# One-tile first block, raw-weight Q and K, split first scores and gate tiles moved into attention

## The chip, the cores and the metric

The kernel runs on one core of a Trainium2 chip. The metric is the device time of one execution in microseconds (us). A core has five instruction queues that run side by side and meet at semaphores: PE (TensorE: matmuls; PEld is its weight load, which overlaps the matmuls), ACT (ScalarE), DVE (VectorE), POOL (GpSimd) and SP (SyncE, which here issues DMAs only). Each queue executes in its own order. Matmul results go to PSUM, which the kernel uses as eight banks of 128 x 512 float32; ACT and DVE evacuate them from there to SBUF.

## The reference

One transformer-like block on 2048 tokens of width 448: adaptive layer norm, sliding-window attention with 16 heads of width 28 (window 256), then a second adaptive layer norm and a gated MLP whose gate mixes tokens with a 2048 x 2048 matrix.

```python
mod = silu(c) @ w_mod                      # 6 vectors of 448: sa ca ga sb cb gb
h = layernorm(x) * (1 + ca) + sa
q, k, v = split(h @ wqkv)                  # 16 heads of 28
s = q @ k.T * 28 ** -0.5                   # causal, |q - k| < 256
x = x + ga * ((softmax(s) @ v) @ wo)
h = layernorm(x) * (1 + cb) + sb
z = gelu(h @ w_in)                         # 1792 wide
z1, z2 = z[:, :896], layernorm(z[:, 896:])
g = w_sp @ z2 + b_sp[:, None]              # w_sp: 2048 x 2048
x = x + gb * ((z1 * g) @ w_out)
```

## The kernel before

Tokens are cut into 16 tiles of 128. The work is described as small operations (names below), each with its engines, dependencies and the buffers or PSUM banks it takes. `ORDER`, a string of operation numbers, fixes the order of issue on every queue and the choice of engine and bank; nothing is scheduled at run time. Waits follow from dependencies and from buffer reuse.

**Loads.** All on SP's queue except c and one half of the first modulation weights, which ACT's queue issues. Weights with 448 rows are held as four chunks of 128 rows that overlap (`load_dup`, rows 0, 128, 192 and 320), with half of chunk 2 zeroed in the Q, K and V weights (memsets `zv`, `zqk`).

**First layer norm and projections.** Tiles are taken in blocks: `'blocks': (2, 2, 2, 2, 4, 4)`. For each block `ln1` takes statistics (DVE, L543 to L550), the inverse root on POOL (L551) and the normalised tile xn (L565 on DVE, L564 on POOL, L594 on ACT). The first four blocks are transposed by PE (`transp_pe`) and evacuated with the modulation applied: hT, two chunks of 256 columns per operation pair (ACT L622, DVE L626). The last two blocks are transposed by DMA (`transp_dma`, L641) and modulated afterwards (L633). The modulation columns modT come from 32 one-column matmuls (`mod_cols`) on the first load of w_mod. `project` then runs, per block, eight chains of four matmuls for Q and K (QKT, heads in four groups of 32-row slots), evacuated at L718 (ACT) or L721 (DVE), and one chain of four per tile for V (Vaug, L729 or L732). The Q and K weights are first copied from wqk_raw into WQK with each head widened from 28 to 32 columns (`wqkp`, L657 and L658, eight copies over three engines); every chain of Q and K waits for such copies.

**Attention.** Query tile j meets key tiles j-2, j and j-1. For each pair one group of 16 matmuls (K = 28, four row groups side by side) writes scores S for all 16 heads into two pairs of banks (bank pairs (0,1), (2,3), (4,5)). Two exponentials (ACT L796, 128 x 1024) each read a pair of banks and write a PT buffer; POOL masks where needed (L804); eight PV matmuls per PT buffer accumulate the output in bank 6. Then rec and nrm (DVE), a DMA transpose to oT, four `wo` matmuls, and x1 (DVE L842). There are 90 exponentials. Banks 6, 7, 4 and 5 (`d_banks`) also serve the projection chains, so scores and projections share banks 4 and 5.

**Gate.** The second layer norm works on x1 in pairs of tiles (h2, by DMA transpose). z2 of a tile is seven passes of 448 columns (`Pair`: six full matmuls and two half-height ones that run side by side), evacuated by the gelu (L899), which needs another ACT table than the exponential. Tiles in `'zraw': (0, 1)` are evacuated without gelu (`z2e`, L892) into z2 and get the gelu later from SBUF (L895). z1 is computed transposed (L918). In the order of this kernel all z1 and z2 matmuls stand behind the last score.

**Mixing.** G: 448 matmuls of 512 columns with the DMA-transposed w_sp, then `ga`, `gu` (DVE), 112 output matmuls, `fin` and the stores.

PE also gets 44 `warm` matmuls of 256 columns and 64 of 128 columns on 32-column groups (16 at a time), on zeros, where the order has nothing else for it; 11 of the 44 stand behind the first score.

Of the kernel before, what the change touches and what calls it, by code (L numbers as in the profile page):

```python
# [55 lines left out]
class Planner:  # L56
# [108 lines left out]
0 16 7 1 21 20 17 18 26 23 28 27 118 120 2 3 1673/0 1674 1675 1676 1677 1678 1679 1680 1681 1682 1683 1684 1685 29/2 1686 1687 1688 1689 1690 1691  # L165
1692 1693 1694 25 30 1695 32/1 33 34 31 8 9 14 6 10 5 4 12 15 13 11 50 119 51 121 54 52 122 53 19 22 55 123 24 56 58/0 124 57 125.2/4 126.2/1 35 1696
1697 1698 1699 1700 36 37 1701 60/0 38 1702 1703 39 59/3 127/0 131/2 40 41 49 46 45 48 47.1 128 61 62.1 63.1 65/1 1704 64 1705 1706 132 1707 1708 1709
66 67 134 129.1 130.1 42 43 44 323 319 321 325 324 326 320 322 327 93/3 88/7 98/0 89 90 103/2 104 99 100 101 91 94 83/1 105 68/6 69 106 70 84 102 92
107 133 85 71 78/7 86 79 95 96 80 81 87.1 72 97 73/0 74 82 75 76 113/6 114 115 116 252 185 77 487/0,1 488/3 491/6 328 329 330.1/1 117.1 333.1/4
332.1/3 489 492 331.1/2 1710 108/4 109 110 1711 140/1 111 141 142 1712 1713 143 145/0 146 147 1714 1715 1716 148 502/1,0 112 155/2 156 157 158 186 254  # L170
253 255 187 402 188 189 404 159.1 403 256 144 149 485/1 135/0 136 1717 137 138 1718 165/2 166 167 168 506/0 503/1 486 509/0,1 139 169 493/0 490 170/2
171 1719 1720 172 180/1 181 182 183 173 160/3 161 162 163 510/7 512/9 184 522/0,1 150/1 151 152 153 494 495/1 257 258 507 504 190 408 406 174.1 191
334 336 337 496/1 335 154.1 505/0 513 511 508 407 514 515/2 405 164 526/10 523/3 529/1,2 530/7 192.1/3 193.1/0 259.1/4 175/1 176 177 178 179.1 516/0
533/1 194/0 195 409 196 197 536/0,1 198/1 199 200.1 201.1 222/3 497/2 498 499 500 207/0 223 208 209 210 224 202/1 203 225 539/4 537/5 211 226 549/0,1
553/8 550/6 260.1/1 531 410 501 932 265/2 204 205 206.1 212/3 232/0 213 214 215 233 266 234 235 216.1 517/1 518 519 520 227/3 521 534 524 411 412 554
527 413.1/3 415.1/0 236 268 267 556/1,0 560/0 557/9 228 229 230 538/0 237/2 217/1 525 238 239 231.1 934 218 219 262/3 261 220 240 532 535 340 241.1
221 264.1 263.1 563/1,0 540 528 564/2 566/4 269/1 242/3 314/2 243 270 315 316 317 244 245 576/1,0 541 933 935 542/2 318.1 936 246.1 577/5 580/3 294/0
295 271 272 296 247/2 297 279/3 248 249 280 281 250 273.1 274/1 275 276 282 277 419 543/1 903 900 902 901 298.1 283.1 278.1 251 583/1,0 284/0 299/2
300 301 302 285 286 287 584/7 587/10 303.1 289/1 290 291 292 288.1 590/1,2 591/1 416.1/2 561 558 414.1/1 551 418 339.1 937 341.1 567/0 555 552 938
293.1 939/2 581 578 941/0 588 585 338.1 559 565 562 593/6 603/1,0 544/1 545 546 547 607/8 604/4 568 569/2 548 917/0 918 919 920 921 922 610/2,0 611/9  # L180
# [43 lines left out]
"""  # L224

PARAMS = {
    'blocks': (2, 2, 2, 2, 4, 4),
    'by_pe': (1, 1, 1, 1, 0, 0),
    'ln1': (-40, -30, 0.3, 3.633, 3.0, 6.5),
    'tr': (-40.674, 0.2, 0.83, 0.9, 3.1, 2.821),  # L230
    'pj': (-38.951, 0.3, 0.8, 1.6, 4.0, 7.776),
    'st': (0.1, 0.1, 0.2, 0.22, 0.407, 0.505),
    'gateA': 0.5,
    'modB': -0.497,
    'gateB': 15.054,
    'pv': -0.964,
    'wo': -19.98,
# [33 lines left out]
def dve4_ns(n):  # L271
    return 225 + n / 3.84
# [811 lines left out]
```

## Time and profile before

| | us |
|---|---|
| runs of the kernel | 282.6, 280.43, 279.98 |
| median of the runs | 280.43 |
| span of the profiled execution | 279.1 |
| busy: PE, PEld | 268.0, 142.8 |
| busy: DVE, ACT, POOL | 156.1, 135.4, 94.2 |
| 90 exponentials on ACT | 84.4 |
| first score, last score (start, PE) | 17.32, 109.89 |
| first exponential, end of the last one | 17.77, 112.5 |
| last matmul ends | 276.3 |

The span runs from the first to the last instruction of one profiled execution; the runs are timed separately and lie a little above it. Busy time is the union of an engine's instructions. A matmul is drawn to its modelled end, so two matmuls back to back overlap in the drawing (a 512-column matmul is drawn 379 ns long), and the distance from start to start in a dense run tells more than a duration does. The granted clock of TensorE was 1.00 in all stretches but the last 20 us, where it was 0.99.

### The profile page before, as it was taken

What the parts mean: (1) busy time and instruction counts of PE and PEld (TensorE: products, weight loads), DVE (VectorE), ACT (ScalarE), POOL (GpSimd) and SP (SyncE); (2) the same over time, 40 slices, a digit from 0 to 9 for tenths busy, and PEclk for the clock granted to TensorE, in tenths of its full rate; (3) what the DMA queues carried; (4) which work ended last, traced back from release to release, by engine and by line L of the source; (5) the groups of instructions that cost most, each with busy time, mean ns of one, the idle gap of its engine ahead of it and who ended that gap; (6) DMA issues with size and microseconds to landing.
All of it is one profiled execution on the core that took longest, in us unless ns stands there. A gap on an engine that the chain in (4) does not pass through costs nothing.

```text
span 279.1 us, 6498 instructions
## 1 busy us (share of the span) xinstructions
PE 268.0 (96%) x2750; PEld 142.8 (51%) x2776; DVE 156.1 (56%) x373; ACT 135.4 (49%) x183; POOL 94.2 (34%) x156
## 2 busy tenths in 40 slices
PE   8899999999999988999999999999999999999995
PEld 4667677655565645444344444444444444444452
DVE  5688775576757688597385841332424230433543
ACT  4689999999999999866566600000000000000000
POOL 4166796755568677646322120000000000000000
PEclk9999999999999999999999999999999999999999
DMA  7954129796587683469999700000000000000223
GB/s 240 366 125 76 23 42 203 131 168 161 145 152 133 126 154 77 94 113 169 172 167 189 133 4 0 0 2 0 0 0 0 19 0 0 2 0 0 66 79 105
DMA packets 67503, 25.38 MB, mean 91 GB/s; under 512 B 56337, under 2 KB 67346, under 8 KB 67474
## 3 DMA queue, kind: packets, MB, share of 16 engines
q1 hardware_dynamic: 67200, 24.50, 42.5%
q8 instruction: 22, 0.36, 0.6%
q10 hardware_dynamic: 274, 0.46, 0.5%
q14 instruction: 7, 0.06, 0.1%
HBM read 9.48 MB, written 1.84 MB: 41 GB/s over the span
## 4 chain that ended last, share of the span: by engine, by line
PE 79%; ACT 16%; DMA 2%; issue 1%; DVE 1%; SPq 0%
PE ps L435 79%; ACT PT L796 13%; DMA wmod_sb<-in_w_mod_dram 2%; ACT hT L622 2%; ACT QKT L718 1%; SPq L466 0%; DVE fin L1005 0%; DVE x_sb L842 0%; DVE st_all L543 0%; ACT Vaug L729 0%
## 5 line engine op out<-in xcount | busy, mean ns | idle before, releaser
L796 ACT ACTIVATE PT<-ps 128x1024 bf16<-128x1024 f32 x90 | 84.4, 1078 | 2.6 <-PE ps L435 2.3
L986 DVE TENSOR_TENSOR tmpg<-ps,bsp_bc 128x512 bf16<-128x512 f32 x28 | 19.3, 691 | 59.2 <-PE ps L435 59.2
L435 PE MATMUL ps<-QKT,z 128*128 128x512 bf16 x219 | 50.7, 379 | 0.3
L804 POOL TENSOR_SCALAR_AFFINE_SELECT PT<-PT 128x512 f32<-128x512 f32 x60 | 37.2, 638 | 11.3 <-ACT PT L796 11.3
L435 PE MATMUL ps<-hT,WQK 128*128 128x256 bf16 (+1 forms) x182 | 34.6, 305 | 2.2 <-ACT hT L622 0.8
L435 PEld LDWEIGHTS ps<-QKT,z 128*128 128x128 bf16 x224 | 21.9, 98 | 26.4
L551 POOL TENSOR_TENSOR rs_all<-ve_all,neghalf 128x1 f32<-128x1 f32 (+2 forms) x31 | 20.0, 650 | 38.1 <-DVE ve_all L550 37.8
L435 PE MATMUL ps<-w_in_sb,hT 128*128 128x448 bf16 (+1 forms) x128 | 29.2, 353 | 0.1
L435 PE MATMUL ps<-hT,w_in_sb 128*128 128x512 bf16 (+1 forms) x106 | 27.5, 379 | 0.5 <-DVE st_all L543 0.3
L435 PE MATMUL ps<-w_spC,z 128*128 128x512 bf16 x110 | 26.7, 379 | 0.1
L435 PE MATMUL ps<-w_spD,z 128*128 128x512 bf16 x109 | 26.1, 379 | 0.2
L435 PEld LDWEIGHTS ps<-Vaug,PT 128*128 128x128 bf16 x720 | 22.7, 97 | 5.8 <-ACT PT L796 0.4
L435 PE MATMUL ps<-Vaug,PT 128*128 128x29 bf16 x720 | 25.0, 176 | 0.5 <-POOL PT L804 0.2
L543 DVE BATCH_NORM_STATS2 st_all<-z2raw 128x6 f32<-128x448 bf16 x32 | 18.6, 615 | 10.4 <-ACT z2raw L899 10.3
L435 PEld LDWEIGHTS ps<-hT,WQK 128*128 128x128 bf16 x192 | 16.9, 97 | 10.8 <-ACT hT L622 1.8
L435 PE MATMUL ps<-w_out_sb,z1T 128*128 128x448 bf16 x112 | 22.3, 352 | 0.0
L633 POOL TENSOR_SCALAR hT<-hT,modT 128x256 bf16<-128x256 bf16 (+1 forms) x31 | 18.5, 601 | 10.8 <-DMA hT<-xn 10.8
L564 POOL TENSOR_SCALAR xn<-x_sb,rs_all,nm_all 128x512 bf16<-128x512 bf16 x23 | 17.5, 769 | 8.0 <-DVE nm_all L555 4.3
L543 DVE BATCH_NORM_STATS2 st_all<-x_sb 128x6 f32<-128x448 bf16 x32 | 18.9, 615 | 1.7 <-DMA x_sb<-in_A_x_dram 1.5
L435 PE MATMUL ps<-QKT 28*128 28x128 bf16 x720 | 18.1, 217 | 1.7 <-ACT PT L796 1.3
L721 DVE CAST QKT<-ps 128x256 bf16<-128x256 f32 (+1 forms) x27 | 14.2, 531 | 8.3 <-PE ps L435 7.9
L918 ACT ACTIVATE z1T<-ps 128x512 bf16<-128x512 f32 x28 | 15.6, 600 | 5.8 <-PE ps L435 5.7
(70 smaller groups left out, 273.3 us busy)
## 6 DMA issues: line engine op xcount, KB each, us to landing
wmod_sb<-in_w_mod_dram SPq DMA_DIRECT2D x8, 224.0 KB, 4.0
w_in_sb<-in_B_w_in_dram SPq DMA_DIRECT2D x8, 224.0 KB, 3.8
out_dram<-fin SPq DMA_DIRECT2D x16, 112.0 KB, 1.7
x_sb<-in_A_x_dram SPq DMA_DIRECT2D x3, 448.0 KB, 8.3
wqk_raw<-in_A_wqkv_dram SPq DMA_DIRECT2D x2, 452.0 KB, 7.3
bsp_bc<-in_B_b_sp_dram SPq DMA_DIRECT2D x1, 512.0 KB, 5.8
x_sb<-in_A_x_dram SPq DMA_DIRECT2D x2, 224.0 KB, 3.3
wmod_sb<-in_w_mod_dram ACTq DMA_DIRECT2D x1, 448.0 KB, 4.5
```

Source lines behind the costliest of these rows:

```text
L435: return e.matmul(out_, lhsT=lhsT, rhs=rhs, start=st, stop=sp, **kw)
L543: st = [dve("%sst%d" % (name, i), prio, dve_ns(D), lambda e, i=i, s_=s_: e.bn_stats(st_all[:, slot, t, i, :], s_()), deps, tens) for i, s_ ...
L551: r = pool(name + "rs", prio, 420 + 148 * n, lambda e: e.tensor_tensor(rs_all[:, slot, t0:t1], ve_all[:, slot, t0:t1], neghalf[:, t0:t1], ...
L564: return e.tensor_scalar(dst, src, rs_all[:, slot, t:t + 1], nm_all[:, slot, t:t + 1], ALU.mult, ALU.add)
L622: return e.activation(hT[:, c_, cols], ps[:, ten.slot, q * 256:q * 256 + 256], ACT.Identity, bias=modT[:, c_:c_ + 1], scale=modT[:, 4 + c_ ...
L633: return e.tensor_scalar(hT[:, c_, cols], hT[:, c_, cols], modT[:, base_col + 4 + c_:base_col + 5 + c_], modT[:, base_col + c_:base_col + ...
L718: return e.activation(QKT[:, g, cols], ps[:, ten.slot, 0:w], ACT.Copy)
L721: return e.tensor_copy(QKT[:, g, cols], ps[:, ten.slot, 0:w])
L796: e_op = P.op("E%d_%d" % (j, ui), pr, [("act", 925, lambda e, ten=ten, pt=pt: e.activation(PT[:, pt.slot, :, :], ps[:, ten.slot:ten.slot + ...
L804: ready = pool("M%d_%d" % (j, ui), pr - 50, pool_ns(512), lambda e, pt=pt, pat=pat, cm=cm, cmp=cmp: e.affine_select(out=pt32(pt.slot), in_ ...
L918: g = P.op("z1g%d_%d" % (tb, ft), pr - 19, [("act", act_ns(512), lambda e: e.activation(z1T[:, ft, tb * 512:(tb + 1) * 512], ps[:, ten.slo ...
L986: a = dve("ga%d_%d" % (tb, ft), pr, dve_ns(512), lambda e, tb=tb, ten=ten, tg=tg: e.tensor_tensor(tmpg[:, tg.slot, :], ps[:, ten.slot, :], ...
```

## The change

Nine things are changed together, and `ORDER` is a new one throughout.

1. Blocks are 1, 1, 2, 4, 4 and 4 tiles instead of 2, 2, 2, 2, 4 and 4. PE transposes the first three (tiles 0 to 3), DMA the rest, so tiles 4 to 7 now come by DMA.
2. All weights of 448 rows in the first half lie in four chunks of 112 rows, without overlap (`load_112`, R1 = 112); xn is written in four chunks of 112 with 16 columns of padding, zeroed once (`xpad`). The memsets `zv`, `zqk` and the copies of c fall away. The loads of x are 1, 3, 4, 4 and 4 tiles; wqk is loaded ahead of wv; on ACT's queue the half of wmod stands ahead of c.
3. Q and K of the first block are made from wqk_raw without the widening copy: each matmul of a chain becomes four with 32 columns of weights, one for each column group (`raw_chain`).
4. A widening copy waits for its half of wqk_raw only.
5. For j = 0 the scores come in two halves of eight matmuls, for head groups (0, 1) into banks 0 to 3 and (2, 3) into banks 4 to 7, each with its own exponential.
6. hT chunks are evacuated per transposed bank; in the first two blocks 112 x 128 each.
7. `zraw` is tiles 0 to 4 instead of 0 and 1, and ordering constraints that kept gate work behind certain scores are dropped. By the new order z2 of tiles 0 to 3 stands ahead of the last score.
8. All 44 warm matmuls now stand ahead of the first score.
9. In attention ACT has eight 512-column copies of QKT instead of five.

```diff
-    'blocks': (2, 2, 2, 2, 4, 4),
-    'by_pe': (1, 1, 1, 1, 0, 0),
+    'blocks': (1, 1, 2, 4, 4, 4),
+    'raw': (1, 0, 0, 0, 0, 0, 0),
+    'by_pe': (1, 1, 1, 0, 0, 0),
...
-    'zraw': (0, 1),
+    'zraw': tuple(range(5)),
...
-    x0 = load_x("x0", -99, 0, 2)
-    t_wmA = load_dup("wmodA", -98, wmod_sb, w_mod, 0, 2 * D, engs=("sp", "act"), rate=290.0)
-    t_wv = load_ov("wv", -97, wv_sb, A_wqkv, 2 * D, 3 * D, o=2 * D)
-    x1 = load_x("x1", -96, 2, 2)
-    t_wqk = load_dup("wqk", -95.5, wqk_raw, A_wqkv, 0, 904)
+    x0 = load_x("x0", -99, 0, 1)
+    t_wmA = load_112("wmodA", -98, wmod_sb, w_mod, 0, 2 * D + 16, engs=("sp", "act"))
+    t_wqk = load_112("wqk", -97, wqk_raw, A_wqkv, 0, 904)
+    x1 = load_x("x1", -96, 1, 3)
+    t_wv = load_112("wv", -95, wv_sb, A_wqkv, 2 * D, 3 * D, o=2 * D)
...
+        def raw_chain(g):
+            ten = Ten(B_D if b else B_ALL, guard=True)
+            ops = []
+            for k in range(4):
+                def fn(e, k=k):
+                    last = None
+                    for r in range(4):
+                        a = 112 * g + DH * r
+                        last = mm(e, ps[32 * r:32 * r + 32, ten.slot, 0:w], wqk_raw[0:R1, k, a:a + 32], hT[0:R1, k, cols],
+                                  k == 0, k == 3, tile_position=(0, 32 * r))
+                    return last
+                ops.append(pe("qk%d_%d_%d" % (b, g, k), 0, mm_ns(w), fn, [t_wqk[k // 2], hT_op[b][k]], [ten], order=ops[-1:], mode=33))
...
+                s_ops = []
+                halves = [[Ten(banks((a, a + 1))) for a in a_] for a_ in ((0, 2), (4, 6))] if j == 0 else [tens]
+                for gs, tens in zip(((0, 1), (2, 3)) if j == 0 else ((0, 1, 2, 3),), halves):
+                    deps = [QK_op[(g, blk[j])] for g in gs] + [QK_op[(4 + g, blk[kb])] for g in gs]
+                    s_ops.append(pe("S%d_%d%s" % (j, ui, "h%d" % gs[0] if j == 0 else ""), pr - 50, 270,
+                                    lambda e, j=j, kb=kb, tens=tens, gs=gs: s_mm(e, j, kb, tens, gs), deps, tens, mode=32, order=all_S[-1:]))
...
-                    [pair.ops], [joint, zt], table="gelu", order=[prev_e])
+                    [pair.ops], [joint, zt], table="gelu")
```

More of the change, by code (lines that the diff above doesn't have):

```diff
@@ L602, in transp_pe @@
         hT_op[b] = [None] * 4
-        for half in range(2):
+        per = 1 if b == 0 else 2
+        for u in range(4 // per):
             ten = Ten(B_ALL if b == 0 else B_D, guard=True)
@@ L799, in bass_adaLN_cond__sliding_block__mixer_gmlp__prompt_kernel @@
+            S_op[(j, ui)] = s_ops[-1]
+            e_op = P.op("E%d_%d" % (j, ui), pr, [("act", 925, lambda e, e_in=e_in, e_out=e_out: e.activation(
+                e_out(), e_in(), ACT.Exp, scale=SCALE))], [s_op, t_exp0], e_tens + [pt], table="exp")
             E_op[(j, ui)] = e_op
-            e_op.scores = -1
             ready = e_op
```

323 lines of the change are left out of this document (162 added, 161 removed), and 4 rows, old and new, of the table PARAMS.

## The prediction

> **What bounds the kernel now.** I read the stages first (busy time of each engine in chosen stretches; the numbers after the range are its length, then busy us and instruction counts of PE, PEld, DVE, ACT, POOL, then clock, DMA share, GB/s).
>
> ```profile
> 17.30:30.00 12.70, 12.22 (x213) 8.64 (x213) 11.13 (x30) 12.06 (x18) 10.39 (x16) 1.00 0.35 66
> 30.00:75.00 45.00, 43.91 (x817) 28.70 (x826) 30.91 (x73) 43.66 (x54) 30.39 (x47) 1.00 0.66 127
> 75.00:95.00 20.00, 18.98 (x410) 11.67 (x404) 12.57 (x29) 19.88 (x23) 13.40 (x22) 1.00 0.70 134
> 95.00:105.00 10.00, 8.97 (x196) 5.47 (x194) 8.65 (x16) 9.56 (x11) 8.15 (x15) 1.00 0.90 161
> 105.00:110.60 5.60, 4.76 (x125) 3.49 (x122) 4.71 (x12) 5.54 (x7) 4.09 (x7) 1.00 0.37 77
> 110.60:160.00 49.40, 49.03 (x283) 21.16 (x288) 33.92 (x93) 33.23 (x52) 20.82 (x35) 1.00 0.83 147
> 160.00:276.30 116.30, 115.73 (x543) 53.86 (x551) 42.10 (x85) 0.45 (x1) 1.58 (x3) 1.00 0.04 14
> ```
>
> TensorE (PE) is full almost everywhere: it stands still 1.6 us from 17.3 to 75, 2.9 us from 75 to 110.6, 0.9 us after that. ACT is as full as PE until 110. So time comes off in three ways: an earlier start, less PE work, or filling PE's 2.9 us. The chain of waits (start, length, what) agrees: late in attention it runs over the exponentials, after it over PE alone.
>
> ```profile
> 80.62 23.95 ACT PT L796 x26
> ...
> 110.56 5.83 PE ps L435 x57
> 116.39 0.05 issue
> 116.44 9.28 PE ps L435 x49
> ```
>
> The start, from the timeline (start, length, engine, line, instructions, and in brackets the idle time before and its releaser):
>
> ```profile
> 7.99 0.47 PEld L435 LDWEIGHTS ps<-sc_sb,wmod_sb 128*128 128x128 bf16 x16 [1.01 <-DMA wmod_sb<-in_w_mod_dram]
> 10.62 0.63 ACT L658 ACTIVATE WQK<-wqk_raw 128x512 bf16<-128x512 bf16 x1 [1.02 <-DMA wqk_raw<-in_A_wqkv_dram]
> 11.15 3.28 ACT L622 ACTIVATE hT<-ps,modT 128x256 bf16<-128x256 f32 x7
> 14.49 2.14 PE L435 MATMUL ps<-hT,WQK 128*128 128x256 bf16 x18 [0.56 <-ACT hT L622]
> 17.32 0.40 PE L435 MATMUL ps<-QKT 28*128 28x128 bf16 x16
> 17.77 1.94 ACT L796 ACTIVATE PT<-ps 128x1024 bf16<-128x1024 f32 x2 [0.72 <-PE ps L435]
> ```
>
> The modulation weights land at 7.95, ACT evacuates seven of the eight hT chunks one after another until 14.4, the first score is at 17.32, the first exponential at 17.77.
>
> **Paces used**, from dense runs of the timeline: 512 columns 0.216 us (28 matmuls from 168.57 to 174.61); 448 columns 0.19 (8 from 91.20 to 92.81); 256 columns 0.110 (18 in 2.14, less one drain of 0.17); 128 columns 0.056 (10 transposes in 0.72, less the drain); PV 0.027 (48 from 93.15 to 94.53); 16 scores 0.34, and about 0.1 to enter them (four 512-column matmuls took 0.99 ahead of a score, not 0.87).
>
> **1. The first score comes earlier: -4.0 us (-4.7 to -2.7).** Each half of wmod is 408 KB instead of 459 KB behind the same x bytes; 6.14 us of flight scale to 5.5, so it lands near 7.4, not 7.95. 32 one-column matmuls (16 took 0.55) and two copies of 0.15 give modT at 9.0. crow now goes out behind wmod on ACT's queue: that half took 4.5 us from issue, so c is there near 5.5, the silu near 6, the table load of 1.28 ends by 7.6; hidden, as nothing needs ACT before xn1. On DVE, a copy of wqk_raw stands ahead of hT; it needs the first half only. Before, both halves were there at 10.62; the bytes say the first at 9.1 to 10, I take 9.4. Then copy (0.27), modT, three 128-column evacuations: no row has that width; 0.23 (half of the 256-column 0.46) to 0.46, taken 0.34: hT of tile 0 complete at 10.7, its second weight half at about 10.3. Twenty raw groups of four 32-column matmuls follow. The nearest row is the warm-up's: 16 such weight loads in 0.35, 0.55 until the next kind starts; so 80 cost 1.75 to 2.75 us, taken 1.9. With twelve 128-column matmuls (0.7) the half score starts at 13.3. The same row says that a 32-column load at 22 ns is nearly as dear as the full 128-column load of PV at 30. [...]
>
> **2. PE's work from there on: +1.6 us (+1.1 to +2.9).** Q and K before: 96 x 0.110 + 64 x 0.216 = 24.4. After: 12 raw groups (0.09 each) + 20 x 0.056 + 32 x 0.110 + 96 x 0.216 = 26.5. Four more V matmuls fall behind the first score, +0.8; eleven warm-ups no longer do, -1.2; eight transposes fewer, -0.4; three mode changes, +0.3. The upper end takes raw groups at 0.14 and mode changes at 0.4 (the weight-load gap at a warm-up batch).
>
> **3. Waits that the start adds: +1.7 us (+0.5 to +3.5).** The second half score takes all four projection banks (4 to 7). It needs chains for g = 2, 3, 6, 7, one of which waits for the first exponential to free bank 2 (near 15.0) and another for ACT's copy behind that exponential; so it runs near 16.6. By 16.0 ACT has done its two hT chunks of tiles 2 and 3 (0.46 each) and then waits about 1 us. Behind it PE's queue holds one V chain, then K of tile 1, which needs the second exponential to finish (18.0); score 1 needs that K's copy: 19.2. From 15.0 to 19.2 PE has 2.8 us of work: 1.4 us lost. Next, tiles 4 to 7 come by DMA transpose now: statistics on DVE until 17.8, the 4-wide rstd on POOL 1.0, four normalisations of 0.77 until 22.4, four transposes on SP (three took 4.45 to issue, each 2.8 to land), two modulations of 0.77 on POOL: 28.5; PE reaches them at 27.7. With 0.8 there and 0.5 of old idle (12.70 - 12.22), +1.7.
>
> **4. Four gate tiles in attention: -3.6 us (-4.3 to -2.9).** The program says five tiles; by the order of instructions, 32 of 128 matmuls, four tiles, stand ahead of the last score, the fifth behind it. Per tile 6 full and 2 half-height matmuls, 7 x 0.19 = 1.33, so 5.3 us leave the stage after the last score and 16 PV matmuls (0.4) enter it. In attention these 5.3 us fill idle time: 2.9 by the table; up to 4.3 when the runs from 75 to 110 are priced by the paces, as the drawn end of a matmul hides part of a wait. What fits is gain, the rest only changes place. Their eight evacuations (0.55 to 0.62; one on ACT, seven on DVE, which was 8.65 of 10 busy from 95 to 105) lie beside this; the w_out scaling there (3.7 us of DVE) is earlier in the new order. Without that cover each late evacuation would hold a bank, 0.6 us.
>
> **5. Two full engines side by side: +0.6 (0 to 2).** ACT has 1.0 us more evacuations within attention (eight 512-column copies for five, five Vaug for three). At tile 13 the replay puts PE at 95.5 and ACT at 95.6; engines so equal wait for each other.
>
> Cleaned-up orders, 112-row layouts and the moved memsets leave matmul counts as they are: 0. Output and everything from 160 on are unchanged: 0.
>
> **Sum:** -4.0 + 1.6 + 1.7 - 3.6 + 0.6 = -3.7 us against the profiled span of 279.1: 275.4. The median of the runs, 280.43, is 1.3 above that span; the forecast is 276.7.
>
> **Rivals.**
> A, the start gives all back: PE waits 4 us more instead of 1.7 before tile 3, since banks 4 to 7 and the second exponential hang together. For: it's a ring of waits through one engine each. Against: PE has V and projections to do. 276.7 + 2.3 = 279.0. Chance 0.13.
> B, the gate matmuls don't fit: they stand in the last six score periods, where PE gets 13.4 us of work against 11.0 of exponentials, and idle time before 98 can't take them. Term 4 shrinks to -0.3: 280.0. Chance 0.12.
> C, PE has more room than its busy row shows, and ACT alone sets attention: ACT waits for PE only 1.7 us in 17 to 105 and weight loads fill just 55 to 68% of attention. Then the last exponential moves with the first (-4.0, +1.0) and the tail is 4.9 shorter: 280.4 - 7.9 = 272.5. Against: priced by paces, 17 to 75 has under half a us free. Chance 0.12. [...]
> D, slower: the four DMA transposes serialise. Before, POOL waited up to 4.0 us for DMA hT<-xn. First issue 20.9, four landings of 2.8 one after another, modulation: 33.7, against PE at 27.7; PE's queue is in order, so scores 2 and 3 wait behind and ACT starves: 6.0 instead of 0.8, 276.7 + 5.2 = 281.9. Every us after 27.7 costs one; it decides against the change from 31.5 on. Chance 0.13.
>
> **How the numbers follow.** The forecast has 0.50. About 1% (2.8 us) is what a measurement here can tell from no change: faster means under 277.6. Of the forecast's 0.50, 0.38 lie there and 0.12 within 1%, with 274.5 to 279 as its own range. C adds 0.12 to faster and A 0.02; A (0.11), B (0.09) and D (0.01) add to the same; B (0.03) and D (0.12) to slower. Faster 0.52, same 0.33, slower 0.15. The range 273.0 to 280.8 takes in A, B and the low bounds of terms 1 and 4, and leaves out most of C and D.
>
> **What would show it.** First score at 12.6 to 14.6 (1). PE idle from first score to 30 about 2 us (3). Last score near 111, and 161.5 us from it to the end instead of 166.4 (4). PE idle under 1.5 us in the last 35 us of attention, with ACT now waiting for PE there. A first score after 15, or a PE wait of over 3 us for DMA-transposed hT near 28, would make the prediction wrong.

## The result, and the profile after

The changed kernel is slower: 290.19 us median of four runs (287.1, 290.94, 289.77, 290.6) beside 281.44 for the kernel before on the same chip (282.6, 280.43, 279.98, 282.44); ratio 1.030, 95% interval 1.023 to 1.037. The forecast was 276.7. The profiled run is the quickest of the four: 287.1 us, span 285.4, against 279.1 before.

The stages after (busy time of each engine in chosen stretches, columns as before; the first and the last but two borders are the first and the last score):

```profile
16.37:30.00 13.63, 12.86 (x233) 8.75 (x232) 12.11 (x32) 12.31 (x23) 6.74 (x12) 1.00 0.40 93
30.00:75.00 45.00, 43.23 (x759) 24.54 (x755) 30.41 (x75) 41.38 (x49) 31.77 (x48) 1.00 0.58 96
75.00:95.00 20.00, 18.58 (x358) 10.70 (x357) 13.67 (x26) 17.34 (x19) 7.94 (x14) 0.91 0.68 142
95.00:105.00 10.00, 8.39 (x162) 4.54 (x160) 7.23 (x12) 8.93 (x11) 7.07 (x12) 0.83 0.79 146
105.00:121.33 16.33, 14.91 (x276) 8.69 (x273) 11.83 (x28) 12.61 (x15) 11.69 (x20) 1.00 0.35 60
121.33:160.00 38.67, 38.12 (x251) 16.56 (x255) 30.73 (x86) 27.95 (x43) 16.20 (x26) 1.00 0.69 137
160.00:282.60 122.60, 121.95 (x576) 56.56 (x585) 49.84 (x102) 5.49 (x8) 3.27 (x6) 1.00 0.21 41
```

Three readings. First, the balance: the first score comes at 16.37 instead of 17.32 (-0.95), first to last score takes 105.0 instead of 92.6 (+12.4), and from the last score to the end it is 161.2 instead of 166.4 (-5.2); sum +6.3. Second, PE stands still 7.0 us between first and last score (length less busy, five rows), 4.2 before; and ACT, full before, waits 11.3 us for PE (2.3 before). Third, the clock column, 1.00 in every row before, is 0.91 and 0.83 from 75 to 105.

The start, from the timeline:

```profile
11.75 3.46 DVE L650 COPY WQK<-wqk_raw 112x512 bf16<-112x512 bf16 x4
...
11.89 1.18 PE L437 MATMUL ps<-hT,wqk_raw 112*32 112x128 bf16 x70 [0.27 <-DVE hT L617]
12.32 2.75 POOL L543 TENSOR_SCALAR xn<-x_sb,rs_all,nm_all 128x448 bf16<-128x448 bf16 x2
...
15.28 0.34 PE L437 MATMUL ps<-hT,wqk_raw 112*32 112x128 bf16 x10 [2.21 <-issue]
...
16.92 1.04 ACT L827 ACTIVATE PT<-ps 128x1024 bf16<-128x1024 f32 x1
```

The 80 raw matmuls begin at 11.89; after 70 of them, in the middle of a group of four, PE stands still for 2.21 us with no releaser ("issue"). In the same time one of DVE's widening copies takes 2.49 us, where the copy before it and the two behind it take 0.28, and POOL's two normalisations take 0.72 and 2.05 us.

Late in attention, the chain of waits (start, length, what), which before ran over the exponentials there:

```profile
81.35 0.39 DVE x_sb L871
81.74 4.33 DMA hT<-xn
...
86.16 0.72 DVE xn L543
86.88 0.57 DVE hT L626
87.45 0.54 DVE x_sb L871
...
88.04 8.09 PE ps L437 x132
```

DVE's queue is in order. A normalisation of the second layer norm (tile 5) waits at its head until a DMA transpose has read the buffer it needs; behind it stands x1 of tile 7, which frees the bank for PE's V matmuls. PE waits 1.42 us. The same happens on POOL at 116.0 (a modulation waiting for a transpose, a mask behind it, 1.42 us); at 99.06 PE waits 1.43 us for ACT. What follows such a wait shows in stretches of 3.41 us:

```profile
86.11:89.52 3.41, 1.99 (x52) 1.24 (x49) 3.12 (x6) 2.24 (x4) 1.26 (x3) 1.00 0.73 179
89.52:92.93 3.41, 3.41 (x65) 1.89 (x62) 1.33 (x4) 2.58 (x3) 0.00 (x0) 0.50 0.46 74
...
113.41:116.83 3.42, 2.00 (x33) 1.00 (x32) 2.15 (x6) 2.39 (x4) 2.03 (x4) 1.00 0.55 52
116.83:120.24 3.41, 3.41 (x81) 2.15 (x80) 2.69 (x5) 1.85 (x3) 3.41 (x6) 1.00 0.19 38
```

Behind the wait at 88.0 (and the one at 99.1) the granted clock is 0.50 for 3.41 us: by an estimate half of that time, 1.7 us, is lost each time. Behind the wait at 116, as long, it stays at 1.00. The runs of the kernel before test the price: in the sessions below 24 of them had a mean clock of 0.999 or 1.000 and took 280.40 us on average, 17 had 0.994, which is what one such stretch gives, and took 282.07, so 1.67 us more. The other runs of the changed kernel had mean clocks of 0.970, 0.982 and 0.970; by the same estimate, (1 - clock) x span, they lost 5 to 9 us in this way, the profiled one 3.4.

### The profile page after: what moved, and what is told of

It reads as the page before. It is cut to its first block, busy times and chain, and to the rows that moved or that the text cites. A ratio compares the mean times of both kernels' runs of the same rounds, so it can differ in the third digit from the quotient of the medians.

```text
span 285.4 us, 6678 instructions
## 1 busy us (share of the span) xinstructions
PE 270.2 (95%) x2840; PEld 139.1 (49%) x2856; DVE 165.8 (58%) x385; ACT 132.9 (47%) x177; POOL 93.0 (33%) x150
## 4 chain that ended last, share of the span: by engine, by line
PE 77%; DMA 8%; POOL 5%; DVE 5%; ACT 2%; issue 2%; SPq 0%; DVEq 0%; POOLq 0%
PE ps L437 77%; DMA hT<-xn 5%; DMA x_sb<-in_A_x_dram 2%; ACT PT L827 2%; POOL PT L833 2%; DVE st_all L522 2%; POOL xn L543 1%; DMA oT<-o_sb 1%; POOL hT L626 1%; POOL rs_all L530 1%; DVE QKT L734 1%; ACT z1T L947 0%; DVE hT L617 0%; DVE mv_all L525 0%; DVE x_sb L871 0%
## 5 line engine op out<-in xcount | busy, mean ns | idle before, releaser
L827 ACT ACTIVATE PT<-ps 128x1024 bf16<-128x1024 f32 x90 | 85.8, 1040 | 11.7 <-PE ps L437 11.3
L437 PE MATMUL ps<-QKT,z 128*128 128x512 bf16 x219 | 51.7, 379 | 0.2
L437 PE MATMUL ps<-hT,WQK 112*128 112x512 bf16 (+2 forms) x160 | 32.3, 326 | 1.2 <-POOL hT L626 1.0
L437 PE MATMUL ps<-w_in_sb,hT 128*128 128x448 bf16 (+1 forms) x128 | 28.3, 353 | 0.2 <-issue 0.2
L437 PEld LDWEIGHTS ps<-Vaug,PT 128*128 128x128 bf16 x720 | 23.3, 97 | 9.6 <-POOL PT L833 2.3
L437 PE MATMUL ps<-Vaug,PT 128*128 128x29 bf16 x720 | 25.7, 176 | 1.5 <-POOL PT L833 1.4
L522 DVE BATCH_NORM_STATS2 st_all<-z2raw 128x6 f32<-128x448 bf16 x32 | 18.7, 614 | 4.5 <-ACT z2raw L928 2.4
L437 PE MATMUL ps<-QKT 28*128 28x128 bf16 x720 | 18.7, 220 | 2.1 <-ACT PT L827 1.4
L734 DVE CAST QKT<-ps 128x512 bf16<-128x512 f32 (+2 forms) x28 | 14.5, 532 | 8.5 <-PE ps L437 8.5
L626 POOL TENSOR_SCALAR hT<-hT,modT 128x256 bf16<-128x256 bf16 (+1 forms) x25 | 15.9, 640 | 10.6 <-DMA hT<-xn 10.5
L947 ACT ACTIVATE z1T<-ps 128x512 bf16<-128x512 f32 x28 | 15.2, 598 | 7.9 <-PE ps L437 7.8
L437 PE MATMUL ps<-wv_sb,hT 112*128 112x448 bf16 x64 | 16.8, 381 | 1.4 <-DVE x_sb L871 1.4
L543 POOL TENSOR_SCALAR xn<-x_sb,rs_all,nm_all 128x448 bf16<-128x448 bf16 (+1 forms) x21 | 17.0, 817 | 2.3 <-DVE nm_all L534 2.0
```

The lines of the kernel that those rows point to most:

```text
L437: return e.matmul(out_, lhsT=lhsT, rhs=rhs, start=st, stop=sp, **kw)
L522: st = [dve("%sst%d" % (name, i), prio, dve_ns(D), lambda e, i=i, s_=s_: e.bn_stats(st_all[:, slot, t, i, :], s_()), deps, tens) for i, s_ ...
L543: return e.tensor_scalar(dst, src, rs_all[:, slot, t:t + 1], nm_all[:, slot, t:t + 1], ALU.mult, ALU.add)
L626: return e.tensor_scalar(hT[:, c_, cols], hT[:, c_, cols], modT[:, base_col + 4 + c_:base_col + 5 + c_], modT[:, base_col + c_:base_col + ...
L734: return e.tensor_copy(QKT[:, g, cols], ps[:, ten.slot, 0:w])
L827: e_op = P.op("E%d_%d" % (j, ui), pr, [("act", 925, lambda e, e_in=e_in, e_out=e_out: e.activation(e_out(), e_in(), ACT.Exp, scale=SCALE)) ...
```

## The experiments

The theories. **Queue heads**: instructions that wait for DMA transposes hold what stands behind them on DVE and POOL. **Clock**: the waits cost again through the half clock behind them. **Gate**: the four gate tiles in attention only change place. **Start**: late statistics, DVE held by POOL, PE's halt. The table gives, for each kernel, the ratio to the kernel before with its interval, and from the profile when the first exponential, the first one of tile 3 and the last one begin; then what half clock cost by the estimate (half the length of its stretches, the idle end left out), and the span.

| kernel | ratio (95%) | first | tile 3 | last | clock | span |
|---|---|---|---|---|---|---|
| before | 1 | 17.8 | 32.3 | 111.4 | 0 | 279.1 |
| changed | 1.030 (1.023-1.037) | 16.9 | 35.9 | 122.9 | 3.4 | 285.4 |
| e1 gate out | 1.070 (1.062-1.077) | 17.4 | 37.9 | 131.9 | 13.6 | 298.3 |
| e2 queue heads | 1.021 (1.013-1.030) | 17.2 | 36.1 | 120.5 | 3.4 | 283.3 |
| e3 start order | 1.041 (1.035-1.048) | 23.0 | 42.0 | 127.2 | 6.8 | 290.8 |
| e4 no small warm | one run, 293.0 us | 17.3 | 40.5 | 128.4 | 8.5 | 291.3 |
| e5 xn on ACT | 1.026 (1.018-1.033) | 16.3 | 35.6 | 122.0 | 1.7 | 286.0 |
| e6 start order 2 | 1.034 (1.027-1.042) | 17.5 | 36.5 | 124.5 | 3.4 | 287.4 |
| e7 = e6 + e2 | 1.027 (1.020-1.034) | 17.7 | 36.8 | 120.8 | 1.7 | 284.9 |
| e8 = e7 + e1 | 1.062 (1.057-1.068) | 17.0 | 38.1 | 129.6 | 13.6 | 295.8 |
| e9 clean start | 1.032 (1.025-1.039) | 18.2 | 39.1 | 126.8 | 8.5 | 290.2 |
| e10 = e2 + filled | 1.035 (1.029-1.041) | 17.8 | 37.5 | 126.0 | 6.8 | 288.8 |
| e11 = e9 + e10 | 1.038 (1.032-1.045) | 18.5 | 39.5 | 126.7 | 6.8 | 290.3 |
| e13 = e2 + idle matmuls | 1.029 (1.022-1.036) | 18.2 | 39.1 | 123.8 | 6.8 | 288.0 |
| e14 = e9 + e4 | 1.037 (1.031-1.042) | 15.2 | 38.9 | 128.1 | 8.5 | 290.6 |
| e15 = e13 + e14 | 1.035 (1.029-1.041) | 15.1 | 38.9 | 125.2 | 3.4 | 288.4 |
| e17 = e15 + two fills | 1.017 (1.011-1.023) | 14.3 | 37.0 | 121.6 | 1.7 | 285.3 |
| e18 = e17, earlier transposes | 1.020 (1.013-1.026) | 14.8 | 36.5 | 120.1 | 1.7 | 282.9 |

Over the changed kernel and its variants the spans reach from 283 to 298 us; less the clock column they lie between 280 and 285. That subtraction is an estimate (where ACT sets the pace, a slow PE may cost less), but by it most of what tells the profiled runs apart is the clock. From run to run the clock of one kernel differs too, so the ratios, not one profile, decide what is faster: only e1 and e8 (slower) and e17 (faster) have intervals apart from the changed kernel's.

**Gate tiles (e1, e8).** The tokens of z2 of tiles 0 to 3 moved in the order:

```diff
   S13_4 ... wo11 wo12 ... S14_4 ... S15_0 ... S15_4 E15_5
-  (between these: z2m0 z2e0 z2m1 z2e1 z2m2 z2e2 z2m3 z2e3)
+  z2m0 z2e0 z2m1 z2e1 z2m2 z2e2 z2m3 z2e3
   z1m0_4 ...
```

> The changed kernel with z2 of tiles 0 to 3 (matmuls and evacuations) put back behind the last score. Theory 'gate does not fit': in the last score periods the gate matmuls only changed place, so the last score comes about 5.3 us earlier (near 116 instead of 121.3), the time from it to the last matmul grows from 161.2 to about 166.4, and the total stays within 1 us (290 median). Theory 'gate fills idle time' (term 4 of the forecast): the total rises by 3.6 us. Theory 'gate does harm': the evacuations on DVE and the extra waits in attention cost more than the tail gains; the total falls by 2 us or more.

> The run before with z2 of tiles 0 to 3 behind the last score again, as in e1_gate_out, now without the two queue-head waits. Theory 'gate fills idle time' (term 4): 3.6 us slower than the run before at the same clock. Theory 'gate does not fit': within 1 us of it. Theory 'gate keeps the clock up': PE stands still in more places late in attention, the clock halves there as in e1_gate_out, and it is 5 us slower or more.

Measured: by the ratios e1 is 3.8% slower than the changed kernel, e8 3.4% slower than e7. In e1 no theory had this: the last exponential comes later, not earlier, and half clock takes 13.6 us, with one stretch of 17 us from 110.5 on. In e8 the third case held. From the last exponential's start to the end e1 has 166.4 us, the changed kernel 162.5. PE's idle time between first and last score is 9.4 us in e1 and 7.0 in the changed kernel, 7.0 in e8 and 5.0 in e7: the gate tiles fill 2.1 to 2.4 us of it. The clock is a part of the rest: without these dense matmuls it is lower (mean clocks of the runs 0.949 to 0.966 in e1, 0.970 to 0.988 in the changed kernel). How large a part one profile can't say. In the profiled runs, less the clock, e8 and e7 are nearly equal (282.2 and 283.2); but the other three runs of e8 had clocks of 0.971 and took 298 to 300 us all the same. Over all runs, less (1 - clock) x span, the medians are 290.1 for e8 and 283.7 for e7, 287.9 for e1 and 283.0 for the changed kernel. By this estimate the gate tiles in attention gain 5 to 6 us besides the clock.

**Queue heads (e2).**

```diff
   DVE:  ... rec9 nrm9 l2_4nm
-        x2_5
         h2m0_1 x1_7 rec8 nrm8
+        x2_5
         ve13 ...
   POOL: ... M14_0 M13_0 M14_3
-        h2m6_0
         M13_3
+        h2m6_0
         l2_8rs ...
```

> The changed kernel with two instructions moved back in their own queues: on DVE the normalisation of tile 5 (second layer norm), which waits for a DMA transpose to free its buffer, goes behind x1 of tile 7 and the normalised output of tile 8; on POOL one h2 modulation goes behind the last mask of tile 13. Theory 'queue heads': PE's waits of 1.42 us at 88.0 and 1.42 us at 116.0 go, and with the first of them the stretch of half clock after it (about 1.7 us lost), so the last score is 3 to 4.5 us earlier and the total falls by as much (286 to 287). Rival 'ACT or other waits take over': the two waits go, others come, the total falls by less than 1.5 us.

Measured: ratio 1.021 against 1.030. PE's waits at 88 and 116 are gone, and with the first one its half clock; the last exponential comes 2.4 us earlier. So the theory held for the waits. Its gain in time is not shown clear of noise, as the two intervals overlap: the wait for ACT that ends at 97.1 stayed, and this time the clock was 0.50 for two stretches, from 96.5 on.

**The start's order (e3, e6).** The one-tile load of x first, statistics of tile 0 first, c and the silu ahead of most warm-ups.

> The changed kernel with another order at the start only: the one-tile load of x and the load of c go first, statistics and inverse root of tile 0 ahead of those of tiles 1 to 3, c_cols and the silu ahead of most warm-up matmuls, the last modulation matmul ahead of the first transpose. Theory 'start order': the statistics begin near 3.5 instead of 5.8, the modulation columns are there at about 9.4 instead of 10.7, the raw matmuls start near 10.6 instead of 11.9, and the first exponential and the total come 1.0 to 1.5 us earlier. Rival 'weights set the start': the second half of the Q and K weights (11.1 us) holds the chains, so the gain is under 0.5 us. In either case it shows whether PE's halt of 2.2 us within the raw groups is there again, and at which matmul.

> As the run before, and the order at the start of e3_start_order with its fault mended: the second half of the modulation weights is again issued first on ACT's queue, then c, then the silu. Theory 'start order': statistics from 3.5 instead of 5.8, modulation columns at about 9.4 instead of 10.7, so the first exponential comes about 1.2 us ahead of e5's, near 13.7, and the time of the run falls by about as much. Rival 'weights set the start': the Q and K weights (second half at 11.1) hold the chains, gain under 0.5 us on e5.

Both missed, by faults of the edits. In e3 the silu, which waits for c, stood ahead of ACT's issue of half the modulation weights; these went out at 6.02 and landed at 15.1. In e6 the matmuls for c stood ahead of most of the warm-ups and waited for c until 5.2; 51 warm-up matmuls ran behind them until 10.5 and held the modulation matmuls (10.49 instead of 8.20). e3 shows one thing by accident: with POOL idle, DVE's four copies took 0.89 us in place of 3.46.

**PE's halt and DVE's copies (e4, e5, e9, e14).** e4 leaves out the 64 small warm-up matmuls, e5 moves two normalisations from POOL to ACT, e9 takes all of POOL's work away from DVE's copies (and puts the one-tile load of x and the statistics of tile 0 first), e14 is e4 and e9.

```diff
-  wqkf1_3.2 wqkf1_0.2 (POOL) ... xn2.1 xn3.1 (POOL) ... xpad va1
+  nh va1 xpad ... wqkf1_3 wqkf1_0 (DVE) ... xn2.2 xn3.2 (ACT)
```

> The changed kernel without the 64 warm-up matmuls of 128 columns on column groups (128 instructions of PE fewer). Theory 'instructions of PE come late': PE's halt of 2.2 us after its 222nd matmul comes as many instructions later, so after about the 222nd matmul again, which is now beyond the raw groups, in the projections behind them; theory 'something at that time holds PE' (the two slow POOL normalisations and the DVE copy of 2.49 us beside it, or the bank): the halt stays in the raw groups, near 13 us.

> The changed kernel with the two normalisations of tiles 2 and 3 (xn) on ACT instead of POOL, ahead of ACT's copies of Q and K; nothing else moves. Theory 'DVE held by POOL': the DVE widening copy of 2.49 us, which ran while POOL did these two (1.37 us each), takes 0.28 us as its neighbours do, DVE's copies of Q and K come 2.2 us earlier, PE's halt of 2.2 us among the chains of the first block goes, and the first exponential comes at 14.7 to 15.2 instead of 16.9; of this 1 to 2 us reach the end. Rival 'loads or PE's instructions': the halt of PE stays at 13 us, the first exponential within 0.5 us of 16.9.

> The changed kernel with a start in which POOL does nothing beside DVE's widening copies: the two POOL copies on DVE, xn of tiles 2 and 3 on ACT, the two memsets at the head of POOL's queue; also the one-tile load of x, the statistics and the inverse root of tile 0 first, and the last modulation matmul ahead of the transposes (c and c_cols stay where they are). Theory 'DVE held by POOL': all seven copies on DVE take 0.28 us, PE's chains of the first block run without a wait for DVE's copies of Q and K, the first exponential comes at 14.5 to 15.5 instead of 16.9 (16.3 in e5). What is left of PE's halt at its 222nd matmul is then not DVE's. Rival 'loads': first exponential after 16.

> e9_clean_start without the 64 small warm-up matmuls of 128 columns, as in e4. Theory 'PE's instructions come late': the halt was behind PE's 222nd matmul in each trace with these warm-ups, and ended at 14.0 to 16.0 us however early the raw groups began; 64 matmuls fewer, the first half score stands ahead of that place, and with no DVE copy held by POOL either, the first exponential comes at 14.3 to 15.3 instead of 16.9 (18.2 in e9). Rival 'loads hold the start': first exponential after 16. The end follows only where the clock stays up.

Measured, as a table of two by two: the first exponential is at 16.92 with both faults, 17.32 without the halt among the raw groups (e4), 18.21 with DVE free but the halt in place (e9), and 15.20 with both removed from there (e14). One alone brings nothing. The other start order of e9 and e14 is not the reason: their raw groups begin at 11.94 and 12.19, no earlier than the changed kernel's. In e4 the 80 raw matmuls run through, and the next chain waits 2.11 us for a copy that DVE could not start:

```profile
12.54 1.30 PE L437 MATMUL ps<-hT,wqk_raw 112*32 112x128 bf16 x80 [0.28 <-DVE hT L617]
15.95 0.84 PE L437 MATMUL ps<-hT,WQK 112*128 112x128 bf16 x12 [2.11 <-DVE QKT L734]
```

In e5 POOL's two remaining copies and its memsets still overlap; one DVE copy takes 1.94 us. In e14 five copies take 1.09 us together, and neither engine waits for the other:

```profile
12.05 1.09 DVE L650 COPY WQK<-wqk_raw 112x512 bf16<-112x512 bf16 x5
...
12.19 1.30 PE L437 MATMUL ps<-hT,wqk_raw 112*32 112x128 bf16 x80 [0.41 <-DVE hT L617]
...
15.20 1.02 ACT L827 ACTIVATE PT<-ps 128x1024 bf16<-128x1024 f32 x1
```

The halt goes with the count of instructions. In every variant of the changed kernel that keeps the 64 small warm-ups, except e3, PE stops behind the 222nd matmul (for 0.2 us in e7 to 2.8 in e11). Without the 64 small warm-ups it does not go away but moves behind the first half score: in e14, e15, e17 and e18 PE stops for 1.1 to 1.2 us behind the 221st matmul, again in the middle of a group and with no releaser, here in e14:

```profile
16.63 0.40 PE L437 MATMUL ps<-hT,wqk_raw 112*32 112x128 bf16 x13
18.20 0.68 PE L437 MATMUL ps<-hT,wqk_raw 112*32 112x128 bf16 x35 [1.17 <-issue]
```

The traces hold the times of the DMA packets too. The changed kernel's page has a queue for instructions:

```profile
q8 instruction: 22, 0.36, 0.6%
```

That is 22 packets of 16 KB; PE has 5696 matmuls and weight loads, 259 for each packet; e13 and e17, which have the most (5768 and 5776), have 23 packets. The first one after the start runs from 12.61 to 13.74 in the changed kernel, and PE goes on at 15.28, 1.54 us behind its end. In all 15 kernels with the halt PE goes on 1.3 to 1.6 us behind the end of this packet, wherever that lies (12.7 in e5, 16.6 in e14). In the kernel before, in e3 and in e4 it ends at 12.9, 13.9 and 17.1 and the 222nd matmul comes only at 20.2, 21.3 and 18.4: no halt. So, as far as the packets show, PE waits for its instructions. Why the packet itself comes at 11.5 in one kernel and at 15.9 in another is not shown, nor which instructions a packet holds. DVE's copies go with POOL's work: one took 2.49 us beside it (changed kernel) and 0.28 without it (e9), five took 1.09 in e14 and four 0.89 in e3; why is not shown.

But in e14 the gain is gone by tile 3 (38.9, later than the changed kernel's 35.9):

```profile
31.45 1.69 POOL L626 TENSOR_SCALAR hT<-hT,modT 128x512 bf16<-128x512 bf16 x2 [4.59 <-DMA hT<-xn]
...
32.42 3.17 PE L437 MATMUL ps<-hT,WQK 112*128 112x512 bf16 x7 [2.15 <-POOL hT L626]
```

Tiles 4 to 7 come out of their four DMA transposes as late as ever, PE's queue has their projections ahead of the last scores of tile 2, and PE waits 2.15 us where it waited 0.79; here the clock fell too (0.50 from 32.1 to 35.5; seven matmuls of 512 columns took 3.17 us, 1.68 in the changed kernel). The halt of 1.17 us at 17.0 lies in the same stretch.

**Combinations (e7, e11).**

> The run before with the two moves of e2_queue_heads as well. If the parts add up: 290.2 - 2 (e5) - 1.2 (e6) - 2.6 (e2, by its ratio) = 284.4 us, the last score near 115.5. Theory 'waits of PE cost twice': where no wait of PE over 1 us is left, the granted clock stays at 1.00 and the time falls further, to 281 or below; where the wait of 1.43 us for ACT ahead of the last score of tile 12 remains, the clock falls to 0.50 behind it.

> Both: e9 and e10 in one. If they add up and no wait over 1.2 us is left: 290.2 - 2 - 2.6 - 3 = about 282.5, near the kernel before (280 to 282); with the forecast's own sum it would be 276.7. If the excess lies in PE's work rather than in waits and clock: not under 285.

e7 (289.26 us, where the parts would have added up to 284.4) has e6's fault in the start and gains only late: from the first exponential to the last 103.1 us instead of 106.0, with the clock at 0.50 only behind the wait for ACT. e11 joins e9's halt and e10's new wait and misses its forecast by 10 us (292.4, forecast 282.5).

**Filling a wait (e10, e13).** First with real work:

```diff
   qk5_7
-  gateB woutg0 woutg2 woutg3
   S12_0 PV11 PV11 PV11 PV11 S12_2
-  woutg1
+  gateB woutg0 woutg2 woutg3 woutg1
   S12_4 PV11 PV11
-  v12
   S13_0 wo8
+  v12
```

> e2_queue_heads with the gateB matmuls (four of 448 columns, 0.9 us) moved from ahead of the first score of tile 12 to ahead of its last one, where PE stood 1.43 us for ACT, and V of tile 12 behind the first two wo of tile 13's first score. Theory 'waits of PE cost twice': that wait shrinks to about 0.5 us, the clock stays at 1.00 around 95 to 105 (0.50 for 6.8 us in e2), and 2 to 3.4 us of time go with it: 283 to 285. Rival 'clock costs nothing, as ACT sets the pace there': same time as e2_queue_heads (286.7) within 1 us, whatever the clock.

A miss: gateB frees the scaling of w_out (3.61 us on DVE), which now stood ahead of tile 11's output on DVE; PE waited 1.95 us for that, and the clock was at 0.50 for 13.6 us in all. Then with 36 idle matmuls on zeros, which write unused columns of the PV bank:

```diff
   S12_2
+  fill11     (36 x 48 columns)
   S12_4
```

> e2_queue_heads with 36 matmuls of 48 columns on zeros ahead of the last score of tile 12, where PE stood 1.43 us for ACT; they write three unused columns per head of the PV bank and change nothing that is read. Nobody's work comes earlier by them. Theory 'clock follows the columns streamed': in the traces so far every stretch of half clock lasts a multiple of 3.41 us and stands on a grid of that length, behind a window in which the matmuls' columns (at 2.4 per ns, a quarter for matmuls of 28 rows or 32 columns) filled less than 0.40; with the wait filled that window rises from 0.38 to above 0.5, the clock stays at 1.00 there, and the time falls by 2 to 3.4 us against e2 (286.7 by its runs, ratio 1.021 to about 1.012). Rival 'the wait itself costs': same time as e2, or later by what the 36 matmuls take.

The stretch that holds the wait and the one behind it, in e2:

```profile
93.12:96.53 3.41, 2.30 (x68) 1.46 (x66) 2.98 (x4) 2.59 (x4) 1.17 (x3) 1.00 1.88 210
96.53:99.94 3.41, 2.86 (x48) 1.50 (x52) 2.33 (x5) 3.24 (x4) 2.80 (x6) 0.50 0.68 145
```

and in e13:

```profile
97.28:100.69 3.41, 3.06 (x102) 2.47 (x100) 2.72 (x4) 2.79 (x4) 1.31 (x3) 1.00 1.08 191
100.69:104.10 3.41, 3.20 (x58) 1.84 (x59) 2.78 (x7) 3.41 (x5) 2.81 (x5) 1.00 1.43 182
```

By the count of the last section the window with the wait is now filled 0.47, a little less than forecast. The score still comes when ACT lets it, but the clock stays up, and from the first exponential of tile 11 to that of tile 14 it takes 18.1 us instead of 20.5. The total did not follow (1.029; the interval overlaps e2's): in e13 the halt at the start was followed by half clock for 10.2 us, in e2's profile by none, and a wait of 1.24 us at 120 was followed by another stretch.

**Waits in the kernel before (e12, e16).** Four, then three waits for memsets on POOL, in the dense last 110 us:

```diff
+    for a_, b_, k_ in GAPS:
+        last = [byname[a_], warm_ops[-1]]
+        for n_ in range(k_):
+            last = [pool("gap%d_%s" % (n_, b_), 0, 530, lambda e: e.memset(warm[:], 0.0), last)]
+        byname[b_].deps += last
```

> The kernel before, with four waits put into its last 110 us, where PE alone sets the time: PE waits there for one, two, three and two memsets on POOL (0.53 us each, begun when the matmuls ahead end), some 25 us apart. Theory 'waits of PE cost twice': the waits are about 0.8, 1.4, 2.0 and 1.4 us, sum 5.6; behind those of over 1.2 us the clock is 0.50 for 3.4 us or a multiple of it, each time 1.7 us lost or more, so the total rises by 5.6 + 1.7 to 5.1 = 7 to 11 us. Rival 'only the wait itself': it rises by the 5.6 us of the waits and the clock stays at 1.00.

> The kernel before with three waits of about 3 us (five memsets each) in its dense last 110 us, where waits of 0.6 to 1.8 us had left the clock at 1.00. By 'clock follows the columns streamed' a dense window goes under 0.40 only with over 2.0 us of standstill in one window of 3.41 us, so two or three of these waits (where they don't fall half and half on two windows) are followed by exactly one window, 3.41 us, at 0.50, 1.7 us lost each: total +9 for the waits and +3.4 to +5.1. Rival 'a wait of over 1.2 us is enough' fell with e12; rival 'the clock there never falls': +9 only.

e12: waits of 0.64, 1.23, 1.81 and 1.53 us, clock 1.00 throughout the profiled run, 286.16 us against 280.36: 5.8 for 5.2 us of waits. The rival held: among dense matmuls such waits cost only themselves. e16 (one run): three waits of 2.97 us; behind two the clock is 0.50 for one stretch, as here,

```profile
202.24:205.65 3.41, 0.44 (x3) 0.21 (x3) 0.00 (x0) 0.00 (x0) 2.62 (x5) 1.00 0.00 0
205.65:209.06 3.41, 3.19 (x8) 1.21 (x8) 0.00 (x0) 0.00 (x0) 0.00 (x0) 0.50 0.00 0
209.06:212.47 3.41, 3.41 (x17) 1.57 (x16) 1.36 (x3) 0.00 (x0) 0.00 (x0) 1.00 0.00 0
```

and behind the first, which falls half and half on two stretches, it is not. The total, 295.86, is 14.8 above the runs of the kernel before beside it; the waits are 8.9, half clock 5.1 (a third stretch lay at 103.25, in attention).

**All repairs (e15, e17, e18).**

> e13 and e14 in one: start without the halt, without the two queue-head waits, the wait for ACT filled. If halt, queue heads and clock are the whole excess over the forecast: 276 to 280 us, faster than the kernel before or equal; if PE's work in attention is under-priced by the forecast: 282 to 285 with the clock at 1.00.

> e15_all_fixed with 60 more idle matmuls of 48 columns in the wait for the DMA-transposed tiles 4 to 7 (2.46 us at 32.5 in e15, with the clock at 0.50 for 3.41 us behind it), and gateB's four matmuls ahead of the last Q and K chain instead of behind it, into the wait of 2.11 us at 97.5 (half clock behind that too). Theory 'clock follows the columns streamed': both stretches of half clock go; the waits themselves stay (the 60 end about when the transposed tiles come), so the first exponential of tile 3 comes at about 37.2 instead of 38.9, the time falls by about 3.4 us against e15 (ratio 1.035 to about 1.023). With the clock at 1.00 throughout, what is left over the kernel before is work and waits: 283 to 286 us. Rival 'the clock falls somewhere else instead': no gain of over 1 us.

> e17_two_waits_filled with tiles 4 to 7 made ready for their DMA transposes earlier: xn of tiles 5, 6 and 7 on DVE (0.39 us each) instead of POOL (0.70 each), the transposes issued in the order 5, 4, 6, 7, and the fill ahead of the first chain of that block cut from 60 to 24 matmuls. In e17 SP issued the four from 22.54 to 28.63, 1.5 us each, and POOL's first modulation began at 31.00, as early or late as with a first exponential 2 to 3 us later. Theory 'tiles 4 to 7 by DMA pin the stage': issue starts near 21.5, the modulation near 29.9, and the first exponential of tile 3 comes 1 us earlier than in e17 (37.0), the total as much (ratio 1.017 to about 1.013). Rival 'PE's projections of the block pin it': tile 3 within 0.4 us of 37.0.

e15 missed both of its cases, at 1.035: the wait for the transposed tiles grew to 2.46 us and another, for DVE, to 2.11, each with half clock behind it. e17, with idle matmuls in the first and gateB in the second, went down by 1.8%, more than expected; its runs had clocks of 0.993, 1.000, 0.999 and 1.000 and lie within 0.9 us. So at full clock, with the first exponential 3.5 us earlier than before the change, the new order with these 96 idle matmuls is still 1.7% slower (1.1 to 2.3), and its three runs at 0.999 or 1.000 (286.3 to 287.2 us) are some 6 us above those of the kernel before at that clock (280.4). The clock is not the whole excess. e18 is in between its two cases: the modulation begins at 30.29 instead of 31.00, tile 3 at 36.48 instead of 36.98 although its first exponential was 0.5 later, and the ratio doesn't tell it from e17. No version beats the kernel before. The table shows where e18's 3.8 us over the kernel before stand: the first exponential comes 3.0 us earlier, from there to tile 3 it takes 21.7 us instead of 14.6 (+7.1), from there to the last exponential 83.7 instead of 79.1 (+4.6, with the gate tiles' matmuls in it), and behind that 162.8 instead of 167.7 (-4.9). For e17 the four are -3.5, +8.1, +5.5 and -4.0. So most of the excess lies ahead of tile 3.

## Why the prediction was wrong

Against the profiled span the forecast was -3.7 and the result +6.3. The 10.0 us between them are 3.1 at the first score and 7.2 in attention, less 0.3 by which the stage after the last score did better than forecast. The median run is 3.1 us longer than the profiled one, and its clock is lower.

**Term 1, first score earlier by 4.0: it failed, by 3.1 us.** The raw matmuls themselves were cheaper than the forecast's 1.9 us: 80 in 1.30 (e4, e14), 16 ns each. 1.2 us went ahead of them: the forecast scaled the flight of the modulation weights by their bytes to 7.4, but they landed at 8.02 (7.95 before); and it gave the statistics no place in this term, but the three-tile load of x now goes first, they began at 5.82 (3.47 before), the last modulation matmul stands behind the first transpose, which needs them, and the modulation columns came at 10.67 instead of 9.0. 1.9 us went behind their start, to PE's halt and DVE's held copies, which the forecast put at nothing. e14 shows that both must go from ahead of the first score for the gain, and that the first exponential then comes 2.6 us earlier than before.

**Term 3, the waits of the start: right for the changed kernel, wrong in what it hides.** The wait for tiles 4 to 7 was 0.79, forecast 0.8, but by two errors that cancel: the tiles were done at 31.7 instead of 28.5 (statistics 2 us later on the held DVE; the transposes, issued 1.3 us apart, each landed 2.5 us after their issue), and PE came 2.5 us later. So the number was right by luck. When the start is repaired the wait appears (2.15 and 2.46 in e14 and e15): rival D's mechanism, hidden until then by the late start. In none of the runs did a gain at the start get past tile 3, whose first exponential came at 35.6 or later (32.3 before); the forecast added terms 1 and 3 as if they were independent.

**Term 4, the gate tiles.** The tail was right: 161.2 us from the last score, forecast 161.5. In attention PE's idle time between first and last score rose from 4.2 to 7.0 us, where the forecast's terms leave 2.9 (4.2 + 1.7 + 0.6 - 3.6). The gate matmuls themselves fill 2.1 to 2.4 us (e1, e8), less than the forecast's 3.6 but not rival B's 0.3; what the forecast left out is the waits that came with the new order. What no part of it had is that with these matmuls the clock stays higher: without them the kernel is about 10 us slower (e1, 300.86 us beside 290.19), of which the clock is a part (0.954 in e1's profiled run, 0.988 in the changed kernel's).

**Terms 2 and 5.** The work is not contradicted: the matmuls between first and last score, priced by the forecast's paces in both orders, are 6.4 us more (the forecast's terms: 1.6 and, of the gate, 5.3 less 0.4). PE's busy time there rose by 9.6 us, and 3.4 of that is half clock. Two engines side by side was priced at 0.6; PE's three waits of 1.4 us behind instructions of DVE, POOL and ACT took 4.3. The signal named for it, PE idle under 1.5 us in the last 35 us of attention, failed (4.4 us from 86 to 121).

**The missing term** is the clock. The forecast read 1.00 in every row and took it as given. By the estimate it cost 3.4 us in the profiled run, in the others 5 to 9. Of the 7.2 us in attention 3.4 are the clock, and the rest, 3.8, is nearly the 4.1 us by which PE's idle time exceeds the forecast's: waits. Rival C fell: ACT did not set attention alone but waited 11.3 us for PE, although weight loads filled no more of the time than before (24.54 of the 45 us from 30 to 75, 28.70 before).

Open: why e17 and e18, with the halt and the held copies gone from ahead of the first score, take 7 to 8 us more from the first exponential to that of tile 3: the work of a block of four, which is projected whole, the transposes' time, the halt behind the 221st matmul and, in both profiles, one stretch of half clock (from 18.7 and 19.2 on) all lie there. The raw chains, the split scores and the block sizes were not undone one by one.

## What to carry to other kernels

Where PE runs small matmuls, watch the granted clock per stretch and not only the waits: a wait of 1.4 us can cost twice there (1.42 us at 88.0 in the changed kernel), while 1.53 us in a dense stage left the clock at 1.00 (e12), and idle matmuls in it can pay (e17). Read the clock of several runs, as one profile shows one draw of it. Before pricing an earlier start, ask what the stage behind it waits for: here the four transposes came at their own time, whatever the start did. When moving a step on an in-order queue, check what its inputs wait for and who stands behind it. Where an engine stands still and nothing releases it, look for the instruction queue's packets.

## What the runs showed of the hardware

In these runs half clock goes with how little of a stretch of 3.41 us the matmuls fill. In the 18 traces with half clock there are 34 places where it begins, and within each trace their distances are whole multiples of 3.413 us, to 0.03 us; it lasts one or more such windows. I counted for each window how much of it the matmuls' columns fill at 2.4 per ns (rounded from the dense pace, 512 in 0.216 us), with a quarter for matmuls of 28 rows or of 32-column weights, a weight chosen because it fits. Of 1437 windows (from 11 us to the last matmul), 56 are filled less than 0.40, and the next window is at 0.50 behind 55 of them (the other is filled 0.397); 1363 are filled 0.44 or more, and none is followed by half clock; of the 18 between, 6 are. The bound of 0.40 was on record ahead of e13 to e18, and they keep to it. PV (eight matmuls of 29 columns in 0.22 us) fills 0.45 at best by this count, and a wait of 1.4 us in a window of PV and scores was enough (0.37 and 0.26 in the changed kernel; 0.43 at 116, where nothing followed). In a dense stretch a wait of 1.81 us was not (e12), and two of 2.97 us were (e16); by the count over 2.0 us of one window are needed there, an estimate. At half clock seven matmuls of 512 columns took 3.17 us (e14), which is 0.47 by this count; attention stayed at 0.50 for up to 17 us (e1), while dense 512-column matmuls left it after one window (e16). The kernel before is near the edge too: 19 of its 43 runs beside the experiments had a mean clock of 0.994 or 0.988, and its variant e16 had a window at 0.38 in attention, with half clock behind it.
